# The first group's raw x: two rounded parts kept in DRAM and added later, in place of a copy out of its bank

## The chip, the cores and the metric

The kernel runs on one core of a Trainium2 chip. The metric is the time of one execution on the device in microseconds (us); the median of several executions counts. The engines are named as in the profile: PE (TensorE matmul), PEld (its weight loads), DVE (VectorE), ACT (ScalarE), POOL (GpSimd) and SP (SyncE, which issues every DMA here).

## The reference, cut to what matters

Attention over 4 batches, 8 heads, 768 positions and 64 columns per head: each query sees the keys less than 16 positions away and 24 summary keys (maxima over blocks of 32 keys; their values are means). Its output, laid out as x of 3072 x 512, goes through a two-layer network with softplus:

```python
scores_all = np.concatenate([scores_l_m, scores_s], axis=-1)
a = np.exp(scores_all - np.max(scores_all, axis=-1, keepdims=True))
a = a / (np.sum(a, axis=-1, keepdims=True) + 1e-09)
attn_out = np.matmul(a, np.concatenate([v, v_sum], axis=2))
...
x = np.ascontiguousarray(attn_out.transpose(0, 2, 1, 3)).reshape(B * S, H * D)
h = x @ w_in                                   # 3072 x 512 by 512 x 2048
g = np.maximum(h, 0.0) + np.log1p(np.exp(-np.abs(h)))
return (g @ w_out).astype(np.float32)          # by 2048 x 512
```

## The kernel before

**Groups and passes.** The 3072 tokens form six groups x = 0 to 5 of 512 tokens, each of two chunks i of 256. Attention of a chunk is done for two head pairs at a time (hp = 0 and 2), so a group has four blocks, called a0.0.0, a0.0.2, a0.1.0 and a0.1.2 for group 0 (group, chunk, hp); block n = 2i + hp/2. Groups 0 to 4 first go through the first half of the 16 feed-forward slices (f = 0 to 7, called f0.0 to f0.7 for group 0), group 5 through all of them, and then groups 4, 3, 2, 1, 0 through slices 8 to 15. The second pass uses another product scheme (`hidden_pair`, with sums and differences of the blocks of x), so it needs each group's x again. PE's products take each fp32 operand as two rounded parts (high, and the rest, low) and sum three of the four products.

**Where x goes.** A block's attention output stands in a PSUM bank, xo. For group 0, `attention` does three things with it: ACT or DVE copies the whole bank into an SBUF tile r (the *take*, L767), SP writes r to DRAM (`keep`, L619), and for each of the two columns of heads ACT copies the bank into the high part of xw (L786) and DVE subtracts that from the bank into the low part (L790). The xw tiles of group 0 lie in the tags x3 to x6, which group 2's xw uses next. In the second pass `attended` (L1339) loads the four raw blocks of a group back into r, and `prepare` makes the operands x0 to x6 from them by differences and splits (L796, L803, L811, L812).

**Attention of a block.** PE scores (L646); a DVE mask with the minimum, eight instructions (L659); ACT exponentials, eight (L667); DVE inverse of the sums (L674, L675); normalization by DVE or POOL (L680) or ACT (L683); PE transposes and ACT copies them to pT (L700, L704; for groups 1 to 5 a DVE transpose L713 and a way through DRAM instead); PE values into xo (L746, L754).

**Weights.** Each pair of slices is loaded, rounded and split in a chain per tile: magnitude (DVE L933 or ACT L936), clamp (L940), shift (L944), sign (L948) on DVE, tail (ACT L954 or DVE L957), add of the tail (POOL L962), high (ACT or DVE L966), low (DVE or POOL L973). The first pair, w0, stands in four tiles of 512 columns, wi0_0, wo0_0, wi0_1, wo0_1; later pairs in tiles of 1024.

**What sets the order.** Every piece of work is a task with a number. The string SEQUENCE lists the 2037 tasks in the order in which they are issued, and so the order of each engine's own queue. A letter behind a number (a, b) takes one of the task's other ways, another engine. Each engine works through its queue in order, and SP through its DMAs. The score bank sc is one buffer, xo and ph share two PSUM banks for the hidden products (`bank`, tag ph), and group 0's xo uses the tag po. 40 short matmuls on the identity (L1298) fill PE's opening.

Of the kernel before, what the change touches and what calls it, by code (L numbers as in the profile page):

```python
# [10 lines left out]
F32 = mybir.dt.float32  # L11
# [130 lines left out]
def pool(n):  # L142
    return 0.17 + 0.00219 * n
# [4 lines left out]
23 124 0 125 2 3 25 4 44 47 5 134 161 6 7 24 8 31 27 9 10 126 130 35 11 127 12 128 13 129 14 26 131 33 50 1 132 133a  # L148
51 15 16 52 17 85 18 135 136 66 19 137 20 138 29 21 22 45 82 162 139 37 163 166 53 32 164 54b 165 39 41 67 167 34 284
48 143 68 36 28 55 30 140 57 88 46 168 69 38 49 89 70 40 56 58 90 104 86 180 169 42 84 141a 105 142a 43 106 291 91 59  # L150
309 148a 92a 144 145 146 83 87 147 152 107 170 71 61 108 171 63 62 73 72 292 74 75 334 338 293 149 64 60a 181 93 182
95 183 316 77 79 184 94 96 97 351 76 80 150a 185 120 199 78 294 295a 153a 109 157 154 111 155 110 156 112 113 296 317
158 101 99 100 176 102 151a 159 218 336 115 117 160a 318 297 342 340 116 227 346 98a 118 186 285 121 335 219 339 228
172 173 174 220 319 358 221 229 222 230 223 376 289 337a 114 320b 234 235 224 175 344 286 204 231 177 298 301 299 290
321 241 343 236 287 300 242 187 237 178 341a 225 243 244 226 179 232 288 322 345 359 189 360 233 123 122 239 190 238
245 347 200a 188 302 310 361 383 201 362b 323 348 314 202 240 248 203 468b 472a 205 363 312 313 249 246 303 469b 467
384 326 324 191a 385 325 315 311 255 195a 206a 192 207 364 208 209 256 193 386 194 247 250 251 257 475 252 196 258 327
494b 259 387b 498a 262 349a 365 368 366 263 352 355 328 350 493 356 197a 269 388 367 198a 210a 270 476 353 357 354 495
253 264 211 389 65 643 265 212 214 213 254 271 266 501 272 215 273 369 519 477 260 377 380 216a 217 378 381 261 520a
478 526 521b 390 393 267 370 307 479a 305 308a 306a 372 392 391 382 480 268 373a 329 379 274 502 481 641 278 645 503  # L160
276 330a 332a 333a 277 275 529 394 547 331 548a 549 374a 375 395 399 482 485 484 470 279 397a 398 400 401 402 504 473
483 103 471 474 505 410 403 404 554a 281 282 405 644 506 411 406 412 413 530 507 407 649 647 408 414 409 531 557 486
# [12 lines left out]
762a 631 935a 765 852 763a 837 766 775 635a 767 851 768 875 769 916 876 776 777 940a 770 632 778 633 943 853 877 634
917 879 1028 779 638a 782 542 854a 863 880 639a 1027 636 866 1029 902 771 878 783 918 919a 772 868 869 864 920 944 789
773 945 784 1032a 946 790 785 774 855 735 786 903 780 947 791 792 856 865 781 787 921 881 793 1359 908 904 948 949
1035 882a 1036 1037 1038 1039 922 911 796 797 640 1040 803 804 798 805 914 924 909 1052b 806 799 1056a 858 913 925
1053 800 923 1051 788 794 795 801 637 910 1059 859 807 761 1060 886a 1076 926 936 950 927a 953 942 802 808 809 929
931a 1077a 939 1082a 857a 932 928 810 811 1061 941 1075 884a 885 812 813 937 817 818 814 951 952 815 819 938 1041 1062  # L180
954 820 955 1493 709 1085 1063a 1030 930 816 957a 1360 887a 959 821 1042 956 1045 822 1031 1034 1044 1064 826 960 958a
824 1102 961 825 962 963 1101 970 1033 964 883 829a 1108a 830 971 972 823 1043 973 1065 1086 1103 965 974 1111 1046
1087 827a 1054 966 1047 967 1088 1049 1050 1057 1055 1361a 1089 1048 1066 968 1058 1069 977 978 979 980 984 985 981
986 1090 1112 987 1068 831 969 991 992 993 1494a 988 1067 994 995 1091 975 1070 1365 828 1362 1113 1114 1071 1073 1499
976 1078 1074 1092 1084 982 983 1072 998 999 1495 1093 1005 1000 1095 1369 1001 1115b 989 1079 1081 1080 1083 1002 990
1116 1006 1094 1096 1007 1117 1008 1099 996 1104 997 1106 1009 1105 1012 1366 1097 1118 1013 1372 1003 1014 1110 1121
1015 1016 1120 1100 1109 1107 1496 1004 1119 1010 1503 1098 1500a 1011 1018 1019 1122 1017 1123 1125 1124 1021 1024
1126 1127 1128 1136 1129 1137 1020 1130 1138 1131 1185 1022 1132 1143 1144 1139 1186a 1140 1150 1203 1145 1025 1151
1204 1133 1205 1134 1187 1221 1188 1189 1206 1152 1146 1135 1153 1147 1154 1208a 1141 1207 1226 1194 1157 1142 1164
1165 1158 1222 1199a 1370a 1209 1190 1148 1026 1149 1210 1155 1212 1240 1023 1195a 1223 1224 1196 1225 1213a 1197 1198  # L190
1200 1191 1159 1227 1160 1166 1192 1156 1230 1211 1161 1167 1193a 1168 1171 1172 1241a 1242 1228 1178 1173 1174 1217a
1243 1162 1231 1163 1179 1244 1278 1229 1259 1175 1236 1245 1232a 1233 1214 1169 1234 1201 1235 1180 1246 1181 1170
1182 1295 1260a 1261 1176 1296 1215 1302 1237 1262 1283a 1303 1177 1249 1297 1298 1216 1299 1183 1304 1184 1250 1247
1264 1268 1218 1305 1306 1309 1219 1371a 1310 1316 1202 1263 1238 1248 1265 1220 1311 1312 1317 1300 1255 1318 1301
1266 1239 1307 1308 1269 1313 1279 1280a 1319 1270a 1251a 1320 1267 1323 1281 1252 1253 1274 1324 1254 1325 1326 1327
1330 1271 1256 1314 1331 1272 1337 1332 1373a 1338 1333 1315 1273 1334 1282 1344 1374 1345 1287a 1339 1367 1257 1368
1340 1258 1375 1321 1322 1363 1341 1364 1328 1329 1378 1275 1276 1376 1346 1347 1348 1379 1380a 1501a 1284 1377 1335
1381 1384 1382a 1385 1383 1387 1386 1388 1389 1392 1390 1277 1336 1391 1288 1285 1393 1396 1397 1394 1395 1403 1286a
1342 1404 1343 1349 1351 1289 1502 1398 1405 1408 1290a 1410 1411 1409 1350 1506 1353a 1412 1352 1356a 1417 1414 1357
1415 1419 1399 1413 1420 1418 1358 1421 1354 1400 1509a 1423 1401 1416 1355 1422 1424 1428 1429 1425 1402 1430 1406  # L200
1433 1436 1439 1435 1434a 1437 1440 1438 1442 1441 1444 1446 1291 1407 1426 1445 1443 1627 1448 1447 1449 1453 1454
1497a 1450 1455 1427 1292 1293 1458 1294a 1431 1461 1459 1462 1464 1460 1463 1469 1498a 1465 1467 1471 1466 1470 1468
1472 1473 1478 1479 1504a 1489 1633 1630 1474 1507a 1505a 1432 1451 1452 1508a 1456 1457 1485 1510a 1475 1480 1512
1513a 1637 1511a 1514a 1515 1517 1516 1518 1521 1519 1520 1524 1525 1528 1522 1523 1526 1628 1629a 1476 1477 1527
# [27 lines left out]
def kernel(  # L232
# [9 lines left out]
    nc = tc.nc  # L242
# [379 lines left out]
    def attention(x, i, hp, tiles, by_pe):  # L622
# [136 lines left out]

        order.add(PE, 1.6 if tiles.sums else 1.2, values, [pT, *((pT, k) for k in range(NSQ)), *tiles.v_keys], [xo])  # L760

        r = None
        if x < NX - 1:
            r = block(2 * i + hp // NG)

# [6 lines left out]
            if x:  # L772
                return r
# [623 lines left out]
```

## Time and profile before

| | |
|---|---|
| time, median of 3 runs | 614.34 us (614.16 to 617.19) |
| the profiled execution's own time | 613.83 us |
| its span, first to last instruction | 612.0 us |
| PE busy | 602.7 us (98%) |
| DVE, ACT, POOL busy | 379.3, 343.3, 180.6 us |
| granted TensorE clock | 1.000 |

The profile is that of one execution. A busy engine is one with an instruction in it; PE's matmuls overlap, so a matmul that took 0.39 us on average is followed by the next after 0.23 us. All windows are in us from the first instruction. A number in square brackets behind a timeline row is the idle time of that engine just before, with what ended it.

### The profile page before, as it was taken

The numbers are of one execution on the slowest core, as the hardware profiler recorded it, in microseconds if no ns is written. First come the engines' busy times: TensorE is split into PE (matmuls) and PEld (weight loads), VectorE is DVE, ScalarE is ACT, GpSimd is POOL, SyncE is SP. The second block draws the span as 40 slices with busy tenths as digits, with TensorE's granted clock in tenths as the row PEclk, the third lists the DMA queues.
The fourth block names the chain that finished last, engine by engine and source line by source line (L and its number), as shares of the span: only waits on it lengthen the run. The fifth ranks groups of instructions, "written<-read, shape, count | busy, mean of one in ns | idle before, by whom it ended". The sixth has DMA issues, their size and how long they took to land.

```text
span 612.0 us, 12214 instructions
## 1 busy us (share of the span) xinstructions
PE 602.7 (98%) x4575; PEld 505.6 (83%) x4575; DVE 379.3 (62%) x992; ACT 343.3 (56%) x846; POOL 180.6 (30%) x178
## 2 busy tenths in 40 slices
PE   8899999999999999999999999999999999999997
PEld 7567878888788888888888888899898989999996
DVE  4999987846465665442235689854765655554543
ACT  4989998986778656576266986432213222233211
POOL 4445255134115132210003553572411216012000
PEclk9999999999999999999999999999999999999999
DMA  8999778966868576665428520041040230020121
GB/s 304 310 314 250 236 238 258 280 193 230 263 196 263 175 213 225 213 201 193 135 75 270 206 70 1 1 155 52 2 172 2 103 138 1 35 103 1 48 92 69
DMA packets 66714, 96.13 MB, mean 157 GB/s; under 512 B 5888, under 2 KB 44896, under 8 KB 65888
## 3 DMA queue, kind: packets, MB, share of 16 engines
q1 hardware_dynamic: 66656, 95.36, 48.1%
q8 instruction: 36, 0.59, 0.4%
q14 instruction: 22, 0.18, 0.1%
HBM read 66.06 MB, written 27.26 MB: 152 GB/s over the span
## 4 chain that ended last, share of the span: by engine, by line
PE 86%; DVE 11%; ACT 2%; issue 1%; POOL 0%; DVEq 0%; ACTq 0%; POOLq 0%
PE po L1224 40%; PE ph L1059 21%; PE hx L1099 10%; PE hy L1099 7%; PE xo L746 4%; PE sc L646 3%; DVE sp L659 1%; PE warm L1298 1%; DVE t L948 1%; DVE t L940 1%; DVE ks L352 1%; DVE w L973 1%; DVE gl L1217 1%; DVE tb L713 1%; DVE t L944 1%
## 5 line engine op out<-in xcount | busy, mean ns | idle before, releaser
L1224 PE MATMUL po<-w,gh 128*128 128x512 f32 x766 | 202.7, 392 | 0.3 <-DVE w L973 0.3
L1224 PEld LDWEIGHTS po<-w,gh 128*128 128x128 f32 x766 | 141.0, 188 | 29.6 <-DVE w L973 0.7
L1059 PE MATMUL ph<-xw,w 128*128 128x512 f32 x672 | 161.9, 392 | 0.2 <-POOL w L973 0.2
L1059 PEld LDWEIGHTS ph<-xw,w 128*128 128x128 f32 x672 | 125.1, 188 | 28.1 <-POOL w L973 0.7
L1224 PE MATMUL po<-w,gl 128*128 128x512 f32 x383 | 114.5, 392 | 0.6 <-DVE gl L1217 0.6
L1224 PEld LDWEIGHTS po<-w,gl 128*128 128x128 f32 x383 | 70.7, 188 | 15.3 <-DVE gl L1217 1.0
L667 ACT ACTIVATE sp<-sp,nm 128x120 f32<-128x120 f32 x192 | 73.1, 384 | 5.9 <-DVE nm L659 5.7
L1209 ACT ACTIVATE gh<-hx 128x512 fp32r<-128x512 f32 x20 | 12.0, 600 | 107.6 <-DVE hx L1109 107.6
L962 POOL TENSOR_TENSOR t<-t,raw 128x1024 int32<-128x1024 int32 (+1 forms) x20 | 40.8, 2044 | 103.9 <-DVE t L948 70.0
L1217 DVE TENSOR_TENSOR gl<-ph,gh 128x512 fp32r<-128x512 f32 x56 | 38.2, 686 | 53.0 <-ACT ph L1213 52.8
L1209 ACT ACTIVATE gh<-ph 128x512 fp32r<-128x512 f32 x56 | 33.4, 598 | 37.7 <-PE ph L1059 37.3
L803 POOL TENSOR_TENSOR x<-r,x 128x512 fp32r<-128x512 f32 x23 | 30.5, 1339 | 67.9 <-DVE x L796 58.2
L659 DVE CUSTOM_DVE_ANT_0 sp<-sc,added 128x120 f32<-128x120 f32 x192 | 40.8, 278 | 5.9 <-PE sc L646 4.9
L667 ACT ACTIVATION_READ_ACCUMULATOR sp<-sp,nm 128x1 f32 x192 | 36.2, 189 | 0.0
L1099 PE MATMUL hx<-x,w 128*128 128x256 f32 x240 | 35.7, 285 | 0.0
L1099 PE MATMUL hx<-x,sw 128*128 128x256 f32 x240 | 35.5, 284 | 0.0
L1099 PEld LDWEIGHTS hx<-x,w 128*128 128x128 f32 x240 | 32.9, 190 | 2.1
L1099 PE MATMUL hy<-x,sw 128*128 128x256 f32 x240 | 34.4, 284 | 0.0
L1209 ACT ACT_TABLE_LOAD x23 | 29.5, 1283 | 6.3 <-PE ph L1059 5.9
L1213 ACT ACTIVATE ph<-ph 128x512 f32<-128x512 f32 x56 | 32.9, 591 | 0.0
L1099 PEld LDWEIGHTS hx<-x,sw 128*128 128x128 f32 x240 | 32.0, 190 | 0.8
L1099 PEld LDWEIGHTS hy<-x,sw 128*128 128x128 f32 x240 | 31.2, 191 | 0.2
(122 smaller groups left out, 828.0 us busy)
## 6 DMA issues: line engine op xcount, KB each, us to landing
squares<-tb SPq DMA_DIRECT2D x20, 512.0 KB
pT<-squares SPq DMA_DIRECT2D x80, 128.0 KB
raw<-w_out_dram SPq DMA_DIRECT2D x16, 512.0 KB
kf<-kT_dram SPq DMA_DIRECT2D x16, 384.0 KB
raw<-w_in_dram SPq DMA_DIRECT2D x6, 1024.0 KB
q<-qT_dram SPq DMA_DIRECT2D x20, 256.0 KB
raw<-r SPq DMA_DIRECT2D x20, 256.0 KB
part<-ob SPq DMA_DIRECT2D x10, 512.0 KB
```

Source lines behind the costliest of these rows:

```text
L646: nc.tensor.matmul(unit(g * NU + h * NPAIR + i)[r * QW:(r + 1) * QW, k0:k1], lhsT=q[rows, w * QW:(w + 1) * QW], rhs=k[rows], start=True, s ...
L659: nc.vector.tensor_tensor_reduce(out=sp()[:, n], in0=unit(n), in1=added()[:, kinds.index((lows[w], lows[w + 1]))], scale=-SCALE, scalar=FL ...
L667: nc.scalar.activation(sp()[:, n], sp()[:, n], AF.Exp, bias=nm()[:, n:n + 1], scale=-1.0, accum_out=ss()[:, n:n + 1],)
L746: nc.tensor.matmul(xo()[h * D:(h + 1) * D, g * CH + w * QW:g * CH + (w + 1) * QW], lhsT=v[:, h * D:(h + 1) * D], rhs=queries(g, w, h)[:KW ...
L803: engine.tensor_tensor(to(1), a(), to(0).bitcast(F32), op=ALU.subtract)
L962: nc.gpsimd.tensor_tensor(a, a, word(0, I32), op=ALU.add)
L1059: nc.tensor.matmul(ph(), lhsT=lhs(part, cc), rhs=xw[cc][0]()[:, xw[cc][1], a], start=cc == 0 and n == 0, stop=cc == NCC - 1 and n == 2,)
L1099: nc.tensor.matmul(to()[:, half], lhsT=lhs(wa, cc), rhs=of_x(xa)[:, cc * CH:(cc + 1) * CH], start=cc == 0 and m == 0, stop=cc == NG - 1 an ...
L1209: nc.scalar.activation(gh(), all_of(), AF.Softplus)
L1213: nc.scalar.activation(all_of(), all_of(), AF.Softplus)
L1217: nc.vector.tensor_sub(out=gl(), in0=all_of(), in1=gh().bitcast(F32))
L1224: nc.tensor.matmul((to or po[t])()[:, c0:c1], lhsT=a()[:, t * P:(t + 1) * P], rhs=w2()[:, part, i2 * DM + c0:i2 * DM + c1], start=(f == f0 ...
```

## The change

The take of group 0's four blocks and the four `keep` writes of 256 KB are left out. In their place `keep_parts` writes each of the four xw tiles (high and low parts of both chunks) to DRAM, 512 KB each, and in the second pass `summed` loads, for each block, both parts of two tiles (two DMAs of 256 KB in rows of 1024 B) into a tile named both and adds high and low into r. The tile both takes the tag tb for the blocks n = 0 and 2 and the tag pT for 1 and 3, one buffer each. The four adds are on POOL.

The new SEQUENCE has 2041 tasks; its first 616 positions, which reach to about 155 us of the profile before, are arranged anew, and behind them the order is the old one but for the new loads and adds. Within the stretch up to the low part of the last block of group 0 these are the differences in the queues, read off the numbers:

- PE: 15 instead of 12 of the identity fillers stand ahead of the scores of a0.0.0. The first products of f0.0 stand ahead of the values of a0.1.2, not behind them, and the hidden products of f0.2 ahead of the first projection of f0.0.
- From DVE to ACT: the magnitudes of wi0_0, wo0_0, and of the 1024-wide tiles wi1 and wi2; the high parts of wo0_0 and wi0_1.
- From ACT to DVE: the tail and the high part of wi0_0; from ACT to POOL: the normalization of a0.0.0; later the high part of wo0_1 from ACT to DVE.
- From POOL to DVE: the normalization of a0.1.0 and a0.1.2, the low part of wo0_0, and later that of wo0_1. From DVE to POOL: the normalization of a1.0.0.
- DVE: two of group 1's key maxima (L352) come ahead of the low parts of a0.0.2 and a0.1.2, not behind them.
- ACT: the exponentials of a1.0.2 stand ahead of the high parts of a0.1.2, not behind them.
- SP: the loads of wo0_0 and wo1 are issued later, the last two key loads of group 0 earlier. The writes of the parts stand where the old keeps did, among the DMAs of groups 1 to 3.

```diff
 SEQUENCE = """
-23 124 0 125 2 3 25 4 44 47 5 134 161 6 7 24 8 31 27 9 10 126 130 35 11 127 12 128 13 129 14 26 131 33 50 1 132 133a
+0 23 121 2 3 25 44 47 4 5 6 83 7 27 29 8 9 157 24 10 11 12 13 122a 123 31 126a 14 15 33 124 16 17 26 125 127 80 50
...
-        r = None
-        if x < NX - 1:
+        if 0 < x < NX - 1:
             r = block(2 * i + hp // NG)
...
-            if x:
-                return r
+            return r
         xw = whole_x(x)
...
-        return r
+
+    first_parts = {}
+
+    def keep_parts(cc):
+
+        buf, i = whole_x(0)[cc]
+        first_parts[cc] = to = buffer([P, 2, CT], F32, f"parts{cc}", pool=dram, bufs=1)
+        order.add(
+            SP, 0, lambda: nc.sync.dma_start(out=to(), in_=buf()[:, i].bitcast(F32)),
+            [(buf, i, part, k) for part in range(2) for k in range(2)], [to], size=512 * KiB, row=4096,
+        )
+
+    def summed(n, r):
+        i, hp = n // 2, n % 2 * NG
+        both = buffer([P, 2, NG, CH], F32, "both", ("tb", "pT")[n % 2], 1, work)
+        for g in range(NG):
+            def load(g=g):
+                src = first_parts[hp + g]()
+                nc.sync.dma_start(out=both()[:, :, g], in_=src[:, :, i * CH:(i + 1) * CH])
+            order.add(SP, 0, load, [first_parts[hp + g]], [(both, g)], size=256 * KiB, row=1024)
+
+        def add(engine):
+            to = r().rearrange("p (g c) -> p g c", g=NG)
+            engine.tensor_tensor(to, both()[:, 0], both()[:, 1], op=ALU.add)
+        order.add(
+            POOL, pool(NG * CH), lambda: add(nc.gpsimd), [(both, g) for g in range(NG)], [r],
+            ways=[Way(DVE, dve(NG * CH), lambda: add(nc.vector), port=True)],
+        )
...
-            n = 2 * i + hp // NG
-            keep(0, n, attention(0, i, hp, tiles, True))
+            attention(0, i, hp, tiles, True)
+        for cc in range(hp, hp + NG):
+            keep_parts(cc)
...
-            def load(n=n):
-                nc.sync.dma_start(out=r[n](), in_=kept(x, n)())
-            order.add(SP, 0, load, [kept(x, n)], [r[n]], size=256 * KiB, row=2048)
+            if x:
+                def load(n=n):
+                    nc.sync.dma_start(out=r[n](), in_=kept(x, n)())
+                order.add(SP, 0, load, [kept(x, n)], [r[n]], size=256 * KiB, row=2048)
+            else:
+                summed(n, r[n])
             prepare(x, n, r)
```

## Rows read from the trace of the kernel before

**Rows 1.** Busy us of PE, PEld, DVE, ACT, POOL by stage; clock, DMA share, GB/s.
```profile
0.00:43.00 43.00, 39.13 (x629) 27.94 (x630) 33.96 (x129) 32.90 (x114) 17.56 (x35) 1.00 0.96 313
43.00:50.00 7.00, 6.77 (x57) 4.68 (x58) 6.82 (x26) 6.02 (x22) 5.82 (x4) 1.00 1.00 290
50.00:78.00 28.00, 26.88 (x277) 21.76 (x269) 27.24 (x68) 26.27 (x73) 9.78 (x7) 1.00 0.80 237
78.00:350.00 272.00, 272.00 (x2113) 222.28 (x2112) 153.57 (x485) 193.45 (x499) 72.87 (x81) 1.00 0.67 212
390.00:600.00 210.00, 210.00 (x1310) 189.56 (x1309) 118.09 (x239) 56.31 (x106) 57.01 (x45) 1.00 0.19 66
```

**Rows 2.** Timeline of the opening: start, us, engine, line, operation, [idle before].
```profile
6.08 0.43 DVE L933 TENSOR_SCALAR t<-raw 128x512 uint32<-128x512 uint32 x1 [1.36 <-DMA raw<-w_in_dram]
...
8.40 1.29 POOL L962 TENSOR_TENSOR t<-t,raw 128x512 int32<-128x512 int32 x1 [2.65 <-DVE t L948]
...
9.79 0.42 PE L646 MATMUL sc<-kf,first 64*64 64x96 f32 x8
...
11.35 0.28 DVE L659 CUSTOM_DVE_ANT_0 sp<-sc,added 128x120 f32<-128x120 f32 x1 [2.33 <-PE sc L646]
```

**Rows 3.** Timeline of PE, the first hidden products and the first projection.
```profile
42.89 2.11 PE L1059 MATMUL ph<-xw,w 128*128 128x512 f32 x8
...
52.01 0.50 PE L1224 MATMUL po<-w,gl 128*128 128x512 f32 x1 [0.56 <-DVE gl L1217]
52.35 0.63 PE L1059 MATMUL ph<-xw,w 128*128 128x512 f32 x2
```

**Rows 4.** Timeline of DVE, 27 to 49 us.
```profile
27.99 0.38 DVE L957 TENSOR_SCALAR raw<-raw 128x512 int32<-128x512 uint32 x1
...
34.34 0.68 DVE L767 COPY r<-xo 128x512 f32<-128x512 f32 x1
34.94 0.69 DVE L933 TENSOR_SCALAR t<-raw 128x1024 uint32<-128x1024 uint32 x1
...
38.59 0.42 DVE L966 CAST w<-t 128x512 fp32r<-128x512 f32 x1
...
39.69 1.16 DVE L680 TENSOR_TENSOR sp<-sp,ss 128x960 f32<-128x960 f32 x1
...
46.30 0.68 DVE L767 COPY r<-xo 128x512 f32<-128x512 f32 x1
46.90 0.41 DVE L790 TENSOR_TENSOR xw<-xo,xw 128x256 fp32r<-128x256 f32 x1
47.23 1.80 DVE L352 TENSOR_REDUCE ks<-kf 128x24 f32<-128x768 f32 x2
```

**Rows 5.** Timeline of ACT, 37 to 49 us.
```profile
37.46 0.60 ACT L767 COPY r<-xo 128x512 f32<-128x512 f32 x1
...
48.16 1.28 ACT L1209 ACT_TABLE_LOAD   x1
```

**Rows 6.** Groups by line and shape, 20 to 55 us: count | busy us, mean ns | idle before.
```profile
L667 ACT ACTIVATE sp<-sp,nm 128x120 f32<-128x120 f32 x38 | 14.5, 386 | 0.0
...
L680 POOL TENSOR_TENSOR sp<-sp,ss 128x960 f32<-128x960 f32 x2 | 3.6, 1791 | 5.0 <-DVE ss L675 5.0
```

**Rows 7.** Timelines of DVE, then of POOL, around 360 us.
```profile
358.06 0.68 DVE L973 TENSOR_TENSOR w<-t,w 128x512 fp32r<-128x512 f32 x1
...
359.80 5.76 DVE L973 TENSOR_TENSOR w<-t,w 128x1024 fp32r<-128x1024 f32 x3
...
360.02 3.31 POOL L962 TENSOR_TENSOR t<-t,raw 128x1024 int32<-128x1024 int32 x1 [1.84 <-issue]
```

**Rows 8.** Timelines of POOL, then of SP, in the second pass.
```profile
490.34 1.30 POOL L812 TENSOR_TENSOR r<-r 128x512 f32<-128x512 f32 x1
510.19 2.54 POOL L803 TENSOR_TENSOR x<-r,x 128x512 fp32r<-128x512 f32 x2 [18.55 <-DVE x L796]
...
475.99 1.38 SPq L1339 DMA_DIRECT2D r<-raw  x3
```

More of the change, by code (lines that the diff above doesn't have):

```diff
@@ L153 @@
[L153 to L162, printed above, removed]
@@ new lines @@
+260 78 261 210 491a 208 209 250 267 262 497 211 268 269 365 515 473 256 386 373 374 387 389 212a 213 388 378 376 257
+377 301a 326a 474 263 366 375 368 475a 303 328 329a 516b 522a 264 476 517b 637 304a 370 643 498 273 270 271 499 477
+302a 272 525 390 543 544a 545 327 277 550 278a 466 467 470 391 639 395 393a 394 396 371a 369a 397 398 274a 500 501 478
+479 480 406 399 400 407 401 502 526 469 481 413 402 414 408 640 641 409 275a 503 645 527 649 410 403 415 404 405 482
+638 528 553 504 507 654 642 411 655b 416 661 529a 492 495 505 412 506 418 496 656b 483a 417 487a 485 493 530 554 531
@@ new lines @@
+419 420 421 555 646 279 647 508 556 557 422 664 683 532 535 509 423 425 533 392 518 523 521 424 644 558 665 520 682
+534 524 519 666 427 434 486a 559 428 651 684a 667 115 114 435 426 429 436 430 431 432 650 437 438 536 560 668a 689a
+692 546 548 552 563 441 442 561 562 669 648 652a 551 547 537a 541a 539a 653 693 711a 715 433 513 443 444 712a 445 549
+540 439 710 367 670 440 694 446 564 657 718 736 695 488 696a 448 565 569 542a 697 737b 741 738b 300 449 671 511a 512
+567 568 570a 719 450 276 659 514a 571 451 572 452 447 573 574 453 456 457 454 455 484 672 325 674 580 581 460a 886 458
@@ new lines @@
+679 624 732a 845 929 897 625 837 462 870b 832 626 735 707a 709a 756a 760a 681 733 930b 846 836 834 758a 627 931a 761
+848 759a 833 762 771 631a 763 847 764 871 765 912 872 772 773 936a 766 628 774 629 939 849 873 630 913 875 1024 775
+634a 778 538 850a 859 876 635a 1023 632 862 1025 898 767 874 779 914 915a 768 864 865 860 916 940 785 769 941 780
+1028a 942 786 781 770 851 731 782 899 776 943 787 788 852 861 777 783 917 877 789 1355 904 900 944 945 1031 878a 1032
+1033 1034 1035 918 907 792 793 636 1036 799 800 794 801 910 920 905 1048b 802 795 1052a 854 909 921 1049 796 919 1047
@@ new lines @@
+965 987 988 989 1490a 984 1063 990 991 1087 971 1066 1361 824 1358 1109 1110 1067 1069 1495 972 1074 1070 1088 1080
+978 979 1068 994 995 1491 1089 1001 996 1091 1365 997 1111b 985 1075 1077 1076 1079 998 986 1112 1002 1090 1092 1003
+1113 1004 1095 992 1100 993 1102 1005 1101 1008 1362 1093 1114 1009 1368 999 1010 1106 1117 1011 1012 1116 1096 1105
+1103 1492 1000 1115 1006 1499 1094 1496a 1007 1014 1015 1118 1013 1119 1121 1120 1017 1020 1122 1123 1124 1132 1125
+1133 1016 1126 1134 1127 1181 1018 1128 1139 1140 1135 1182a 1136 1146 1199 1141 1021 1147 1200 1129 1201 1130 1183
@@ new lines @@
+1305 1215 1367a 1306 1312 1198 1259 1234 1244 1261 1216 1307 1308 1313 1296 1251 1314 1297 1262 1235 1303 1304 1265
+1309 1275 1276a 1315 1266a 1247a 1316 1263 1319 1277 1248 1249 1270 1320 1250 1321 1322 1323 1326 1267 1252 1310 1327
+1268 1333 1328 1369a 1334 1329 1311 1269 1330 1278 1340 1370 1341 1283a 1335 1363 1253 1364 1336 1254 1371 1317 1318
+1359 1337 1360 1324 1325 1374 1271 1272 1372 1342 1343 1344 1375 1376a 1497a 1280 1373 1331 1377 1380 1378a 1381 1379
+1383 1382 1384 1385 1388 1386 1273 1332 1387 1284 1281 1389 1392 1393 1390 1391 1399 1282a 1338 1400 1339 1345 1347
@@ new lines @@
+1513 1512 1514 1517 1515 1516 1520 1521 1524 1518 1519 1522 1624 1625a 1472 1473 1523 1627a 1480 1526 1479 1477 1525
+1533 1534 1527 1528 1535 1538 1541 1630 1482 1486 1544 1539a 1542 1487 1540 1547 1478 1543 1631a 1545 1529 1483 1549
+1632 1548 1550 1530 1551 1552 1553 1546 1554 1558 1559 1555 1531 1532 1560 1536 1537 1563 1564a 1569 1566 1567 1565
+1570 1568 1571 1574 1572 1576 1573 1575 1556 1577 1578 1639a 1579 1580 1636 1557 1583 1584 1585 1561 1588 1594 1589
+1591 1597 1590 1562 1592 1598 1599 1593 1640 1641 1595 1601 1602 1596 1581 1600 1582 1603 1637a 1608 1634a 1628a 1488
@@ new lines @@
+1907 1908 1718 1909 1719 1722 1618 1725 1723 1724 1731 1728 1726 1691 1733 1622 1727 1732 1774a 1768 1894 1695 1735
+1775a 1895a 1729 1771 1777a 1736 1734 1730 1737 1738 1696 1715 1716 1720 1899a 1739 1778a 1769a 1742 1743 1744 1772
+1779 1781 1782 1785 1780a 1783 1721 1786 1784 1790 1788 1787 1789 1904a 1791 1792 1753 1793 1740 1741 1794 1795 1796
+1801 1802 1746 1803 1747 1806 1807 1754 1749 1751 1808 1815 1809 1816 1810 1745 1750 1752 1811 1748 1817 1812 1819
+1813 1818 1814 1755 1821 1822 1912a 1820 1823 1826 1827 1797 1905 1798 1799 1828 1800 1804 1831 1837 1832a 1834 1833
```

101 lines of the change are left out of this document (38 added, 63 removed), and 12 rows, old and new, of the table SEQUENCE.

## The prediction

> **What bounds the kernel now.** I read the busy time by stage first [rows 1]. PE is busy for all 272 us between 78 and 350 us and for all 210 us between 390 and 600 us, while DVE and ACT have room there (154 and 193 of 272 us). The reader is to see that a microsecond taken from DVE or ACT in those stretches is worth nothing. The exception is the opening: the first hidden product starts at 42.89 us [rows 3], and until then PE's 39.1 busy us of 43 [rows 1] are partly the identity fillers. From about 20 to 78 us DVE is the engine without room: 6.82 of 7 and 27.24 of 28 us [rows 1], ACT close behind. So I read PE's timeline for the start of the hidden products [rows 3], then the queues of DVE and ACT to see what they hand over late [rows 4, 5], and the opening for where DVE itself waits [rows 2]. After 78 us PE carries any delay to the end unchanged: the forecast is the shift of PE at 78 us.
>
> **Takes, keeps and parts.** Of the four takes two are on DVE, at 34.34 and 46.30 us, each 0.60 us from its start to the next one's (rows overlap by some 0.08 us, so I count starts), and two on ACT, one of 0.60 us at 37.46 [rows 4, 5]. They are the gain: 1.2 us of DVE and about 1.1 of ACT before 78 us. The keeps are SP issues of about 0.46 us each (1.38 for three DMAs of that size [rows 8]); four go, four of twice the size come, so 1 MB more is written, at a DMA share of 0.67 [rows 1], long after xw was made. I cost them at nothing: group 2's first writes into these tiles, which must now wait for the parts' landing, come some tens of us after the last hidden product of f0 has read them. If that cover is gone, ACT's high part waits, and behind it in ACT's queue the next softplus, then PE.
>
> **DVE's queue to the last low part of a0.1.2.** This is what f0.0's second half waits for; before, it ends at 46.90 + 0.41 = 47.31 us [rows 4]. Leaving it: the takes, 1.20; four magnitudes, two of 0.72 (34.94 to 35.66) and two of 0.46, together 2.36; two casts of 512 columns at 0.33, 0.66; the normalization of a1.0.0, 1.08. Sum 5.3. Entering: two normalizations, 2 x 1.08; a tail, 0.29; a cast, 0.33; the low part of wo0_0, 0.60; two maxima ahead of the lows, 2 x 0.87 [rows 4, 7]. Sum 5.1. So the work is the same within 0.2 us: what the takes free is filled.
>
> **DVE's waits.** Before, the opening has one of 1.36 us and one of 2.33 [rows 2], and smaller ones make it some 4.5. After: ACT makes the first magnitude from 6.08 us, 0.70, so the clamp starts at 6.8, and DVE idles from 4.7 to 6.8 (2.1). With tail, shift, a maximum and the sign (0.3 + 0.5 + 0.9 + 0.7) the sign ends near 9.75, where it ended 0.24 us ahead of POOL's 8.40 before; POOL's 1.29 follows [rows 2], and the cast on DVE waits for it until 11.3 (1.6). Three more fillers of 0.43 us move the first scores from 9.79 to 11.08, and the mask from 11.35 to 12.64 (0.9). Later the high of a0.1.0 and POOL's normalization of a1.0.0 (1.79, [rows 6]) add 0.3 each, small ones 0.2. In all 5.4, so 0.9 more; less the 0.2, the last low part ends near 48.0 us, 0.7 late.
>
> **ACT.** Its exponentials cost 14.5/38 x 8 = 3.05 us a block [rows 6]. Four magnitudes and two casts come in; a normalization of eight instructions, a tail, two casts and the takes go: about even. The order puts the exponentials of a1.0.2 ahead of a0.1.2's high parts: these end near 46.5, just before DVE gets to them. On SP the loads of wo1 now stand behind a load of q that waits for the scores of a1.0.2, near 37 us, some 6 us later than before; ACT and DVE first read wo1 near 47, so I cost it at nothing.
>
> **PE.** f0.0's first half can start near 41 us, ahead of a0.1.2's values, against 42.89; but f0.1's second half ends 0.7 late, near 50.2. Then f0.2's products stand ahead of f0.0's projection and need the bank that f0.0's low part frees: after a table load of 1.28 us [rows 5], two softplus passes and DVE's subtraction that is 52.5, a wait of 1.0 us where the old order waited 0.56 [rows 3]. The old order has by then done one projection (0.7 us) more, and starts f0.2 at 52.35 [rows 3] against 52.5 here, so PE is 0.9 late. From there to 78 us DVE is not later still: the two maxima (1.7) and a tail of 1024 columns (0.6) are gone from behind the lows, a low part and a cast of wo0_1 (0.9) come in, and DVE stands about 1.2 us at that subtraction. The sum is 0.9 us.
>
> **The second pass.** Four POOL adds of 1.30 us. POOL is done at 491.6 and then idle for 18.55 us [rows 8]; two of them stand in front of the row at 490.34. The tile both has one buffer for two blocks, so SP holds the third and later loads until POOL has added the first block, near 491.7, and the last pair until about 498; behind these in SP's queue stand an output of the group before and two reloads of partial sums, which are wanted only when that group's slices are through. Cost nothing; POOL's gap of 18.55 us less 5.2 of adds and some 6 of loading leaves about 7 us before it would cost.
>
> [...]
>
> [...]
>
> **Rivals.** *B, the takes' time comes through.* If DVE's early waits stay at 4.5 us, then the 0.9 does not arise, and if the bank wait is covered PE keeps the 1.2 us of DVE and part of ACT's 1.1: 614.3 - 2.2 = 612.1, at best 610.5. For it: the first hidden half is 1.9 us earlier. Against it: DVE's sum. *C, the block of exponentials is exposed.* ACT stands at a1.0.2's exponentials until DVE's mask comes; if that mask starts more than 2 us after its 42.5 us, the whole 3.05 us delays f0's operands: 614.3 + 0.9 + 3.05 = 618.3, slower. POOL's normalization just ahead of it speaks for, its otherwise idle queue against. [...] *E, a late landing of the parts* stops ACT in front of a softplus near 133 us: more than 4 us late is needed, then 1 to 3 us; I count it with C.
>
> **The numbers.** The profiled execution took 613.83 us, 1.8 more than its span of 612.0, and stands 0.5 below the median; the sum is a difference, put on the median: 614.3 + 0.9 = 615.2. My case, between 613.4 and 617.2 (the upper end is the 3.0 us low part on DVE), has a chance of 0.52, B 0.26, C with E 0.17, D 0.05; mine is also the case in which the change frees takes and gains nothing by it. Half a per cent, 3.1 us, is what can be told from no change. Half of B, 0.13, is beyond it; of C, D and E 0.17; the rest, 0.70, is within. For eight in ten the range reaches into B and C: 611.7 to 618.4.
>
> **What would show it.** In the new profile: the mask of a0.0.0 near 12.6 us, DVE's last low part near 48, the first hidden product near 41 with PE waiting 1 to 2 us before f0.0's second half, another 1 us near 52, and PE without idle time from 80 us on; SP's part loads spread from 476 to 499. Wrong would be a last low part before 46.5 (B), a mask of a1.0.2 after 44.5 (C), or PE idle in the second pass (D).

## The result, and the profile after

The changed kernel takes 618.2 us, the median of 20 executions (615.64 to 624.41), against 614.19 us for the kernel before in the same runs: 1.0075 times the time, with a 95% interval of 1.0059 to 1.0091. It is slower by 0.75%. The forecast was 615.2 us and, with a chance of 0.70, a change too small to be told from none; 618.2 lies just inside the range (611.7 to 618.4), but at 4.0 us the change can be told. Of the experiments below, five executions that took over 1.5% longer than the fastest of their kernel are left out of every figure: one of hyb72_fillers, two of four_fillers_less and two of eight_fillers_less.

The profiled execution took 616.54 us, with a span of 614.7 against 612.0. The stages [rows 1] are now these:

```profile
0.00:43.00 43.00, 39.12 (x590) 28.59 (x591) 33.90 (x131) 31.24 (x107) 18.22 (x34) 0.92 0.93 286
43.00:50.00 7.00, 7.00 (x62) 5.11 (x61) 6.15 (x21) 6.97 (x24) 2.73 (x3) 1.00 0.96 330
50.00:78.00 28.00, 27.99 (x303) 22.82 (x304) 26.13 (x69) 27.34 (x74) 9.93 (x7) 1.00 0.79 245
78.00:350.00 272.00, 270.09 (x2097) 219.75 (x2092) 154.41 (x486) 188.64 (x487) 68.50 (x74) 1.00 0.68 215
390.00:600.00 210.00, 210.00 (x1311) 189.61 (x1310) 120.44 (x240) 55.22 (x105) 63.95 (x50) 1.00 0.21 71
```

Two things stand there that the forecast did not have. Between 78 and 350 us PE is idle for 1.9 us, where it had no idle time. And in the first stage the granted clock is 0.92, not 1.00. From 43 to 78 us, the stretch on which the forecast was built, PE waits less than before, not more.

I followed the same product of the hidden layer through both traces. The first of f0.6 starts at 78.70 us, 0.2 us earlier than before (78.89). The first of f1.0 starts at 100.29 (99.97), its second half at 103.06 (101.44), f1.6 at 138.32 (135.82), and the same projection (`po`) near the end of the second pass at 602.74 (599.84). So PE is ahead at 78 us (and 0.4 us at 91), is 2.5 us late at 138 us, and carries that to the end with 0.4 more.

The waits of PE between 80 and 142 us (before, there is none over 0.2 us) name the places:

```profile
PE ph L1084 <- POOL xw L859: 1.0, 1, 1.0
PE po L1249 <- ACT gh L1234: 0.5, 1, 0.5
PE sc L646 <- ACT sp L667: 0.4, 1, 0.4
```

That is 1.9 us of idle time. Counted from a matmul's start to the next one's start, less the 0.23 us of one at full pace, the three stops cost 1.26, 0.70 and 0.55 us: 2.5 of the 2.9.

The first, in the timelines of PE and of POOL:

```profile
98.23 1.05 PE L646 MATMUL sc<-k,q 64*64 64x120 f32 x32 [0.38 <-ACT sp L667]
...
100.29 0.50 PE L1084 MATMUL ph<-xw,w 128*128 128x512 f32 x1
101.78 2.60 PE L1084 MATMUL ph<-xw,w 128*128 128x512 f32 x10 [0.98 <-POOL xw L859]
...
94.80 2.14 POOL L859 TENSOR_TENSOR xw<-r,xw 128x256 fp32r<-128x256 f32 x3 [4.51 <-ACT xw L852]
99.45 0.71 POOL L512 COPY k<-kf 128x288 f32<-128x288 f32 x2 [2.50 <-ACT sp L667]
100.12 1.60 POOL L859 TENSOR_TENSOR xw<-r,xw 128x256 fp32r<-128x256 f32 x2
```

POOL is idle for 2.50 us in front of a copy of keys (L512) into the window tile k, which has one buffer. The profile puts this wait down to ACT's exponentials; in the old order it puts the same copy's wait, of only 0.31 us, down to PE's scores:

```profile
99.12 0.72 POOL L512 COPY k<-kf 128x288 f32<-128x288 f32 x2 [0.31 <-PE sc L646]
```

The scores of the block before read the tile k. In the new order they start at 98.23 us, after PE's wait of 0.38 us for ACT's exponentials, and end at 99.28; the copy follows at 99.45. (The expectation of lows_ahead below speaks of a copy of q that waits for its load. That is a misreading: the load is issued at 99.33 us, just ahead of the copy's start, and behind the same scores.) Behind that copy stand the two low parts of a1.1.0 that f1.0 needs; their high parts were there from 96.30 us. In the old order one of the two ran on POOL at 95.72 and the other on DVE at 100.02. The wait for ACT is of the same kind, in ACT's timeline:

```profile
127.81 1.28 ACT L667 ACT_TABLE_LOAD   x1 [2.39 <-DVE nm L659]
...
132.27 1.28 ACT L1234 ACT_TABLE_LOAD   x1
133.56 1.09 ACT L1234 ACTIVATE gh<-ph 128x512 fp32r<-128x512 f32 x2
```

The mask of a3.0.0 comes late on DVE (127.44 us, before 125.80), the exponentials end at 132.15, and a second table load lies ahead of the softplus that PE waits for at 133.7 us.

The clock, by windows of the opening (PE, PEld, DVE, ACT and POOL busy, then clock, DMA share, GB/s):

```profile
26.00:30.00 4.00, 3.94 (x108) 3.08 (x108) 3.93 (x12) 3.95 (x16) 0.12 (x2) 1.00 1.06 304
30.00:32.00 2.00, 0.80 (x8) 0.55 (x6) 2.00 (x4) 1.98 (x10) 0.00 (x0) 1.00 1.02 269
32.00:34.00 2.00, 1.85 (x38) 1.51 (x40) 2.00 (x18) 2.00 (x6) 1.30 (x1) 0.97 1.11 290
34.00:38.00 4.00, 4.00 (x57) 3.08 (x56) 3.93 (x10) 4.00 (x18) 0.00 (x0) 0.50 0.88 235
38.00:40.00 2.00, 2.00 (x52) 1.95 (x47) 1.97 (x6) 2.00 (x5) 1.00 (x1) 0.50 0.03 8
40.00:42.00 2.00, 2.00 (x27) 1.34 (x24) 1.52 (x2) 0.98 (x3) 2.00 (x2) 0.82 0.96 311
```

PE is idle for 1.35 us ahead of 32.15 us, and from 33.9 to 40.7 us the granted clock is 0.50. The 20 executions differ in this. In six the mean clock is 0.999 or more, and their median is 617.2 us; in the six with 0.990 or less it is 622.8 us. The kernel before had 0.999 or more in 68 of 77 executions in this study. So about 3.0 us of the 4.0 are there at full clock (617.2 against 614.2), and the executions at a lower clock add 1.0 to the median. Those are the nine at 0.992 or less, with a median of 620.1 us. The five at 0.994 to 0.997, the profiled one among them, have a median of 616.5 us and show no cost of the fall. What brings the clock down is shown only in part: PE's idle time in the first 43 us is the same in both kernels (3.9 us, first lines of the stages).

### The profile page after: what moved, and what is told of

The parts are those of the page before. It is cut to its first block, busy times and chain, and to the rows that moved or that the text cites. A ratio compares the mean times of both kernels' runs of the same rounds, so it can differ in the third digit from the quotient of the medians.

```text
span 614.7 us, 12206 instructions
## 1 busy us (share of the span) xinstructions
PE 604.8 (98%) x4575; PEld 507.4 (83%) x4575; DVE 382.0 (62%) x994; ACT 341.8 (56%) x834; POOL 179.4 (29%) x174
## 2 busy tenths in 40 slices
DMA packets 68314, 98.23 MB, mean 160 GB/s; under 512 B 5952, under 2 KB 47008, under 8 KB 67488
## 4 chain that ended last, share of the span: by engine, by line
PE 75%; ACT 12%; DVE 6%; DMA 2%; POOL 2%; issue 1%; SPq 0%; DVEq 0%; POOLq 0%; ACTq 0%
PE po L1249 33%; PE ph L1084 17%; PE hx L1124 9%; PE hy L1124 7%; ACT sp L667 4%; PE xo L746 3%; PE sc L646 3%; DMA raw<-w_out_dram 2%; PE warm L1323 2%; ACT L961 1%; ACT t L961 1%; ACT L1234 1%; ACT raw L979 1%; ACT w L991 1%; ACT gh L1234 1%
## 5 line engine op out<-in xcount | busy, mean ns | idle before, releaser
L659 DVE CUSTOM_DVE_ANT_0 sp<-sc,added 128x120 f32<-128x120 f32 x192 | 40.7, 277 | 4.4 <-PE sc L646 3.5
L680 POOL TENSOR_TENSOR sp<-sp,ss 128x960 f32<-128x960 f32 x10 | 18.1, 1815 | 66.3 <-DVE ss L675 52.0
```

Of the source, the lines that this page charges most:

```text
L659: nc.vector.tensor_tensor_reduce(out=sp()[:, n], in0=unit(n), in1=added()[:, kinds.index((lows[w], lows[w + 1]))], scale=-SCALE, scalar=FL ...
```

## The experiments

All times are medians. "At full clock" means the executions with a mean granted clock of 0.999 or more.

| kernel | us | ratio to before, 95% interval | at full clock | their median, us |
|---|---|---|---|---|
| changed | 618.2 | 1.0075 (1.0059 to 1.0091) | 6 of 20 | 617.2 |
| parts_old_order | 616.9 | 1.0049 (1.0024 to 1.0073) | 6 of 7 | 616.4 |
| takes_new_order | 623.9 | 1.0152 (1.0134 to 1.0170) | 0 of 4 | |
| lows_ahead | 618.8 | 1.0067 (1.0042 to 1.0092) | 2 of 11 | 615.2 |
| three_fillers | 617.5 | 1.0067 (1.0040 to 1.0095) | 6 of 8 | 617.1 |
| mended | 617.3 | 1.0037 (1.0008 to 1.0066) | 5 of 7 | 615.5 |
| parts_at_keeps | 621.0 | 1.0095 (1.0074 to 1.0116) | 0 of 6 | |
| hyb72 | 622.7 | 1.0138 (1.0123 to 1.0152) | 0 of 4 | |
| hyb72_fillers | 622.6 | 1.0132 (1.0112 to 1.0151) | 0 of 4 | |
| parts_early | 613.9 | 0.9984 (0.9966 to 1.0002) | 11 of 12 | 614.0 |
| takes_new_order_fillers | 621.4 | 1.0109 (1.0069 to 1.0149) | 4 of 7 | 620.9 |
| mended_reloads | 617.5 | 1.0044 (1.0021 to 1.0067) | 9 of 12 | 616.6 |
| four_fillers_less | 616.6 | 1.0040 (1.0009 to 1.0071) | 4 of 9 | 614.5 |
| eight_fillers_less | 617.3 | 1.0055 (1.0022 to 1.0088) | 0 of 10 | |

Theory 1 was the waits of the new order behind 95 us, theory 2 the clock, theory 3 the parts themselves.

**parts_old_order.** The changed kernel's functions, the old order of tasks (renumbered), and the writes of the parts put in as two pairs, here `79 78` and `115 114`:

```diff
+389 263 366 303 475a 301 304a 302a 368 388 387 378 476 264 369a 325 375 270 498 477 115 114 637 274 641 499 272 326a
```

> The change's computation (no takes, the parts written and added) in the order of the kernel before; the first pair of part writes stands behind the same SP instruction as in the changed kernel, the second pair some 30 us earlier. Theory 1 (the new order of the first 616 positions costs the time, above all PE's wait for a POOL low part at 100 us and for ACT at 134 us): 612.5 to 614.5 us, nothing lost, no PE idle time over 0.3 us between 90 and 140 us that the kernel before has not. Theory 2 (the granted clock falls in the opening, because PE idles more there): no fall, so the same as theory 1. Theory 3 (the parts themselves cost: 2 MB more of writes and reads, and their issues in SP's queue hold the loads behind them): 616.5 to 618.5 us.

616.9 us, with the clock up: theory 3's figure. Its six executions at full clock spread from 614.7 to 620.2 us, and the profiled one is the slowest of them. In it, all but 0.2 us of PE's waits between 80 and 142 us are for loads:

```profile
PE xo L746 <- DMA pT<-squares: 2.7, 2, 1.9
PE xo L746 <- DMA v<-v_hp_dram: 1.5, 1, 1.5
PE sc L646 <- DMA q<-qT_dram: 0.8, 1, 0.8
PE po L1249 <- ACT gh L1234: 0.2, 1, 0.2
```

The first pair stands on SP at 86.06 us, just behind the write of a transposed block; that block's third reload is issued at 95.01 us, where it was 92.89. The second pair stands at 100.55 us. (The changed kernel has a first pair at nearly the same place, 86.75 us, and there PE waits for no load.) What this leaves open is whether the bytes cost or their place.

**takes_new_order.** The kernel before in the new order:

```diff
-23 124 0 125 2 3 25 4 44 47 5 134 161 6 7 24 8 31 27 9 10 126 130 35 11 127 12 128 13 129 14 26 131 33 50 1 132 133a
+0 23 125 2 3 25 44 47 4 5 6 85 7 27 29 8 9 161 24 10 11 12 13 126a 127 31 130a 14 15 33 128 16 17 26 129 131 82 50
...
```

> The computation of the kernel before (takes and keeps, no parts) in the changed kernel's new order; each take stands behind the first low part or the first transposed copy of its block, as in the kernel before. Theory 1: 617 to 619.5 us, PE waits again 1 us or more near 100 us for a low part on POOL. Theory 2: 616 to 620 us, with a granted clock below 0.995 in some executions. Theory 3: 613.5 to 615 us.

623.9 us, more than any theory said, all four executions at a clock of 0.989 to 0.992. Without a single part, PE waits at the same places by the same amounts, though it comes there 5 us later:

```profile
PE xo L746 <- DVE gl L1217: 1.0, 1, 1.0
PE ph L1059 <- POOL xw L834: 1.0, 1, 1.0
PE po L1224 <- ACT gh L1209: 0.5, 1, 0.5
PE sc L646 <- ACT sp L667: 0.4, 1, 0.4
```

So the waits for POOL and ACT belong to the new order, not to the parts.

**lows_ahead.**

```diff
-302a 272 525 390 543 544a 545 327 277 550 278a 466 467 470 391 639 395 393a 394 396 371a 369a 397 398 274a 500 501 478
+302a 272 525 390 543 327 544a 371a 369a 545 277 466 467 470 391 639 395 393a 394 396 550 278a 397 398 274a 500 501 478
```

> The changed kernel with six words of the order moved: the two low parts of a1.1.0 stand on POOL ahead of the copy of q that waits for its load, the low part of a1.0.2 stands on DVE ahead of its half of that copy, and two copies on DVE stand behind the low parts of a1.1.2. Theory 1: PE does not wait within f1.0 any more and is 1.3 to 1.6 us earlier from 103 us on; 616.3 to 617.0 us by median. Theory 2: 618.2 us, since the clock's opening is untouched. Theory 3: 618 us, the waits go elsewhere.

The edit moves five words. PE's wait for POOL is gone, as theory 1 said:

```profile
PE xo L746 <- DVE gl L1242: 0.5, 1, 0.5
PE po L1249 <- ACT gh L1234: 0.5, 1, 0.5
PE sc L646 <- ACT sp L667: 0.4, 1, 0.4
PE po L1249 <- DVE w L998: 0.2, 1, 0.2
```

But PE's idle time between 78 and 350 us is 2.0 us in this profile (an execution with a mean clock of 0.991), where it was 1.9: other waits, 0.5 us for DVE the longest, stand in its place. The median did not move, 618.8 us; nine of eleven executions ran below full clock. The two at full clock took 614.91 and 615.46, 2.0 us under the changed kernel's 617.2, but they are only two; the five below 0.993 had a median of 621.0.

**three_fillers.** The new words stand ahead of the values of a0.1.0; later words are renumbered.

```diff
-    for _ in range(20):
+    for _ in range(23):
```

> The changed kernel with three more identity products on PE just ahead of the values of a0.1.0, where PE is idle for 1.35 us at 30.8 us. Theory 1: the wait near 100 us is untouched; 616.8 to 617.5 us by median, since only the executions with a low clock gain. Theory 2 (the fall of the clock makes the loss): the granted clock stays at 1.00 between 33 and 42 us, and the time comes to 614 to 615 us. Theory 3: 618 us.

Six of eight executions ran at full clock, where it had been six of twenty, and there the time is 617.1 us: theory 1's figure. In its profile f0.0 starts 2.2 us earlier than before, and PE has lost all of it at 103 us (1.8 us late). This profile is at full clock throughout, and PE is idle there for 3.3 us between 78 and 350 us:

```profile
78.00:350.00 272.00, 268.67 (x2067) 218.37 (x2067) 153.39 (x484) 186.67 (x482) 67.40 (x73) 1.00 0.69 214
```

**mended.** `lows_ahead`, the transpose 558 ahead of 424, and seven fillers.

> The changed kernel with the moves of lows_ahead, with one transpose of a2.1.2 on DVE ahead of f1.3's subtraction (so that the next mask, exponentials and softplus come earlier: the wait for ACT at 134 us), and with seven more identity products on PE: two ahead of the scores of a1.0.0, three ahead of the values of a0.1.0, two ahead of the scores of a1.0.2. Theory 1 and 2 together (the new order's waits after 95 us, and the clock's fall after PE's idle time in the opening, make the whole loss): clock 0.999 or more in most executions, no PE wait at 100 and 134 us, 614.0 to 615.0 us. Either alone: 616 to 617 us. Theory 3 (the parts' writes): 617 us, PE waits for loads.

The wait for POOL and that of 0.5 us for ACT are gone (one of 0.4 us for ACT's exponentials stays), the clock is up in five of seven, and at full clock the median is 615.5 us, 1.6 better than the changed kernel, though the five spread from 614.9 to 619.1. It is not the 614 to 615 that I expected. PE came to a1.1.0's values 1.1 us ahead and then waited there 1.5 us for a transposed block in DRAM, and 0.8 us more near 214 us for another.

**parts_at_keeps.** Each part in the place of one keep, in the order 79, 78, 115, 114 (the lines of SEQUENCE that hold them):

```diff
+258 345a 361 364 362 259 348 351 324 346 489 352 193a 265 384 363 194a 206a 266 472 349 353 350 491 249 260 207 385 79
...
+271 525 390 543 327 544a 545 370a 371 391 395 478 481 480 466 275 393a 394 396 397 398 500 469 479 78 467 470 501 406
...
+647 648 420 556 421 557a 422 664 682 423 424 508 509 518 521 532 115 427 434 428 419 425 426 558 665 520 535 533 523
...
+650 513 666 514a 485a 683 689a 519 524 534 559 435 429 436 430 431 437 438 684b 432 667 668b 692 711a 710 114 536 537a
```

> As parts_old_order, but each of the four part writes stands where one of the four keeps stood, none of them two together behind a transposed block's write. Theory 3a (in parts_old_order it was the pair of writes just behind the block's write that held its reloads up, so the place costs and not the bytes): 613.5 to 614.8 us, no PE wait for a load over 0.5 us between 95 and 120 us. Theory 3b (2 MB where 1 MB was cost wherever they stand): 616.5 to 617.5 us. Clock 0.999 or more in both.

621.0 us, neither theory. Until 130 us PE ran 0.8 us ahead of the kernel before without a wait for a load, so the pairs and their place were indeed what cost in parts_old_order. Then rival E came, in the order where I had not looked for it: a part was issued at 123.86 us, and ACT's rounding of a2.0.2 over the same tile waited for its landing (the first of ACT's waits, 95 to 140 us):

```profile
ACT xw L852 <- DMA parts<-xw: 4.7, 1, 4.7
```

PE stands behind it, by windows:

```profile
130.00:132.00 2.00, 1.21 (x6) 0.67 (x4) 0.00 (x0) 2.00 (x12) 0.00 (x0) 1.00 0.80 315
132.00:134.00 2.00, 0.00 (x0) 0.00 (x0) 0.00 (x0) 1.97 (x5) 0.00 (x0) 1.00 0.01 2
134.00:136.00 2.00, 1.64 (x6) 1.29 (x7) 0.68 (x2) 2.00 (x6) 0.00 (x0) 0.82 0.00 0
136.00:138.00 2.00, 2.00 (x18) 1.25 (x19) 0.89 (x4) 1.26 (x5) 0.00 (x0) 0.50 0.00 0
```

PE is idle for 3.15 us, and then works at a granted clock of 0.50: 5 us in all, from 0.8 ahead to 4.2 behind.

**hyb72 and hyb72_fillers.** The new order up to the first product of f0.5, then the old one as in parts_at_keeps; the second with mended's fillers.

> The changed kernel's order up to the first hidden product of f0.5 (72 us), behind it all that is left in the order of the kernel before, with the parts where the keeps stood. Theory 1 (the loss lies behind 78 us): 613.5 to 614.8 us in the executions with a clock of 0.999 or more, and 3 to 6 us more in those below 0.992, so a median of 615 to 617 us. If the opening itself lost the time: 617 us or more at full clock too.

> hyb72 with the seven identity products of mended. Theory 1 and 2: clock 0.999 or more in most executions, 613.3 to 614.6 us by median, level with the kernel before. If the fillers themselves delay the opening: 615 us or more at full clock.

622.7 and 622.6 us. Both carry the same late part (issued at 126.0 us in hyb72, where PE waits 4.6 us for ACT and the granted clock is 0.69 from 134 to 138 us and 0.50 from 138 to 142), so they say nothing of the end. Up to 119 us hyb72 is 1.2 us behind the kernel before, after being 0.4 ahead at 83 us: even with the old order behind 72 us something of the new one is still missed in that stretch. They were no test of theory 1.

**parts_early.** The four places of parts_at_keeps with the parts in the order in which they are overwritten: the words 115 and 79 change places. Against parts_at_keeps:

```diff
-258 345a 361 364 362 259 348 351 324 346 489 352 193a 265 384 363 194a 206a 266 472 349 353 350 491 249 260 207 385 79
+258 345a 361 364 362 259 348 351 324 346 489 352 193a 265 384 363 194a 206a 266 472 349 353 350 491 249 260 207 385
+115 639 261 208 210 209 250 267 262 497 268 211 269 365 515 473 256 373 376 212a 213 374 377 257 516a 474 522 517b 386
...
```

> As parts_at_keeps, with the same four places but the parts in the order in which group 2 overwrites their tiles: the one that the first rounding of a2.0.2 on ACT waited 4.74 us for now stands at 86 us instead of 124. Theory: in the order of the kernel before the change gains what the takes free, PE runs 0.8 us ahead from 83 us to the end (as parts_at_keeps did until 130 us), the clock stays at 0.999 or more, and no wait of 1 us or more stands between 95 and 140 us: 613.2 to 613.9 us. Rival (twice the bytes written cost somewhere whatever the places): 614.5 us or more.

613.9 us, and eleven of twelve executions at full clock. Its stages:

```profile
43.00:50.00 7.00, 7.00 (x88) 5.11 (x86) 6.90 (x26) 6.97 (x24) 4.73 (x3) 1.00 1.01 304
50.00:78.00 28.00, 26.74 (x256) 21.91 (x256) 27.24 (x67) 25.97 (x73) 11.11 (x7) 1.00 0.77 233
78.00:350.00 272.00, 271.73 (x2084) 221.67 (x2082) 153.59 (x484) 192.58 (x495) 71.58 (x81) 1.00 0.70 216
```

It is the same computation, with the same 2 MB of parts, as the changed kernel, which takes 4.3 us more. PE is 1.4 us ahead of the kernel before at 57 us, 1.1 at 100 us and 0.3 at the end. It is the fastest version of the study, level with the kernel before within the interval. The new order with its parts in these places was not run, so how much of the changed kernel's loss comes from its own two pairs (86.75 and 132.38 us) stays open; takes_new_order shows that the new order loses time without any part.

**takes_new_order_fillers.** takes_new_order with mended's seven fillers.

> takes_new_order (the kernel before with its takes and keeps, in the new order) with the seven identity products of mended, so that the clock has less cause to fall. Theory (the new order costs 2.5 to 3.5 us behind 85 us by its own waits, without any parts): 616.5 to 618.5 us in the executions with a clock of 0.999 or more, the waits of 1.2 us for POOL near 100 us and 0.7 us for ACT near 134 us unchanged. Rival (the new order costs through the clock alone): 614 to 615 us in those executions.

At full clock 617.4 to 622.6 us, and the waits of 1.0 for POOL and 0.5 for ACT unchanged. The new order costs without the clock and without the parts; by more than I expected, since in the profiled execution (622.6 us) waits of 0.6 us near 49 us and of 2.1 near 217 came to it, and stalls of 1.8 us in the opening (last section).

**mended_reloads.** One reload, 369 here, ahead on SP, against mended:

```diff
-496 260 255 261 330 390b 262 352a 265 355 358 368 331 266 371 353 370 359 360 497b 200a 501a 391 201a 272 369 356 479
+496 260 255 261 330 390b 262 352a 265 355 358 368 331 266 371 369 353 370 359 360 497b 200a 501a 391 201a 272 356 479
```

> mended with one reload of a1.1.0's transposed block moved on SP from behind three loads to just behind its sister (it was issued at 84.8 to 84.9 us in three executions of the new order, at 79.7 to 80.8 us in the old one). If that reload is what keeps PE's values of a1.1.0 from starting before 88 us: they start near 87 us with a wait under 0.5 us, PE stays 0.8 us ahead, 614.0 us. If the loads as a whole fill the DMA there: the wait stays at 1 to 1.8 us and the time at 615 to 617 us.

The values of a1.1.0 now start without a wait, so it was this reload that they waited for. But those of a1.0.2 had waited 1.8 us ahead of 78.33 us, and the time is 617.5:

```profile
PE xo L746 <- DVE gl L1242: 1.8, 1, 1.8
```

This wait is for DVE and not for a load: DVE's subtraction `gl`, which frees a bank, ends at 78.27 us. A wait of 1.0 us for a reload stays near 213 us. The 14 executions at full clock of mended and mended_reloads, which both have the moves of lows_ahead, have a median of 616.6 us, only 0.6 under the changed kernel's. So where the new order's waits lie is well shown, and what taking the first ones away is worth is not: PE then comes sooner to others.

**four_fillers_less and eight_fillers_less.** parts_early without its last four or eight identity products; nothing of the output hangs on these. Against parts_early, with four less:

```diff
-    for _ in range(20):
+    for _ in range(16):
```

> parts_early without the last four of the twenty identity products, those on PE between 13.6 and 15.6 us; nothing else waits for them. If PE's idle time in the opening is what the granted clock falls after: PE idle for 1.9 us there, a clock below 0.996 in more executions than the 1 in 12 of parts_early, and those executions 2 to 6 us longer. If it isn't: 0.999 or more in all and 613.9 us.

> parts_early without the last eight of the twenty identity products (10.2 to 12.2 and 13.6 to 15.6 us), so that PE is idle for some 4 us in the opening. [...]

Full clock in four of nine executions and in none of ten, where parts_early had eleven of twelve. With four less, the executions at full clock take 614.5 us and those below 0.993 a median of 620.2. In the order in which the clock had stayed up, taking fillers out of PE's opening is enough to bring it down. The 6 us between the two groups are not the clock's alone: in the profile they hold a stall of 3.43 us as well. And not every fall costs so much: with eight less, five of the ten executions have a clock of 0.994 to 0.997 and take 614.6 to 615.4 us, and the five at 0.989 or less take 619.2 to 623.6. The windows of four_fillers_less:

```profile
26.00:28.00 2.00, 1.11 (x39) 0.81 (x39) 1.97 (x16) 1.95 (x10) 0.72 (x1) 1.00 1.06 286
28.00:30.00 2.00, 0.21 (x8) 0.11 (x3) 1.93 (x4) 2.00 (x12) 0.00 (x0) 1.00 0.93 250
30.00:32.00 2.00, 0.36 (x9) 0.36 (x13) 1.04 (x4) 0.28 (x2) 0.75 (x1) 0.52 0.40 90
32.00:36.00 4.00, 4.00 (x62) 3.34 (x57) 0.00 (x0) 0.00 (x0) 2.27 (x2) 0.50 0.32 94
36.00:40.00 4.00, 4.00 (x40) 3.01 (x37) 2.55 (x19) 2.58 (x9) 0.00 (x0) 0.50 1.00 348
40.00:42.00 2.00, 2.00 (x23) 1.37 (x22) 1.90 (x4) 2.00 (x12) 0.00 (x0) 0.92 0.94 324
```

In PE's timeline the idle time ahead of the fall ends with this row:

```profile
31.64 0.30 PE L646 MATMUL sc<-ks,q 64*64 64x24 f32 x1 [3.43 <-issue]
```

While PE runs at a granted clock of 0.50, DVE and ACT are empty from 32 to 36 us (0.00 us busy each, PE 4.00 of 4). The idle time ahead of the fall is not the missing fillers' own, though, but a stall of 3.43 us later on (last section); why fewer fillers should bring that on is not shown, and kernels with more of them have it too (three_fillers, 1.4 us). With eight less a first fall, to 0.50 from 13.7 to 17.1 us, does follow the fillers' own gap.

## Why the prediction was wrong

**The step that failed** is the one on which the forecast was put: "After 78 us PE carries any delay to the end unchanged: the forecast is the shift of PE at 78 us." It is a statement about the old order [rows 1], and I used it for a new one that reaches to about 155 us. I read the new queues up to the low parts of group 0 and stopped. The loss is made where I did not read: 2.9 us between 91 and 138 us, 2.5 of it at three stops in which PE waits for POOL's queue and ACT's. takes_new_order shows these waits without the parts, lows_ahead takes the largest away by moving five words (other waits come in its place), and parts_early, the same computation in the old order, has none of them and loses nothing. PE's 272 us without idle time spoke of a slack that the old order had there; the new order had spent it.

**The second miss** is that the clock stands in no step. I took PE's waits in the opening as delays only, and the fillers as filling; that the clock can fall to half for 7 to 14 us behind them (0.50 from 33.9 to 40.7 us in the changed kernel, from 30.7 to 44.4 in eight_fillers_less) I did not weigh. The executions in which it falls longest add 1.0 us to the median, and the slowest is 7 us over the median at full clock; how much of that is the clock and how much the idle time ahead of it the times don't tell. The shorter falls, with a mean clock of 0.994 to 0.997, show no cost here.

**DVE's queue.** Right in size: the mask of a0.0.0 starts at 12.03 us (forecast 12.6), the last low part ends at 48.48 (forecast 48.0; it was 47.31, [rows 4]), in an execution with the clock low from 33.9 us. What the takes free is filled again, in the new order. The upper end of the range, 617.2, was put on a low part of 3.0 us on DVE. No run shows that for the two that moved there: they take 0.68 us (at 31.15) and 0.69 (at 50.18). The one low part of 512 columns near that length, 2.94 us, is in both traces, at 360.93 us before and at 363.83 after.

**PE in the opening.** The first hidden product starts at 42.56 us, not 41; in mended, at full clock, it starts at 40.93, so the step was right and the low clock hid it. The waits of 1 to 2 us ahead of f0.0's second half and of 1.0 near 52 us are not there: a0.1.2's values, at 44.13, fill the first, and f0.2 starts at 51.98 against 52.5 forecast and 52.35 before [rows 3]. At 78 us PE is 0.2 ahead where I had it 0.9 late.

**Takes, keeps and parts.** That they cost nothing holds for the bytes (parts_early) but not for any place: the two pairs of parts_old_order cost 2 us of the median at full clock, and one part issued 1.3 us after ACT had come to overwrite it costs 5. The takes are worth 1.4 us at 57 us in the profile of parts_early and 0.3 at the end, which can't be told from nothing.

**The second pass.** Right: PE is busy for 210.00 of 210 us, the four adds take 1.28 to 1.31 us each, and rival D, PE idle in the second pass, is out. One DVE subtraction (L836), at 503.10 us beside the third add, takes 1.50 us where the same one at 488.12 takes 0.69, and PE does not wait for it. The times were off: the last loads are issued at 505 us and not 499, and the adds run from 493.21 to 508.29 us, none of them ahead of the row at 490.34 [rows 8]; it costs nothing all the same. **Rivals.** B did not come, for the order and not for DVE's sum. C's 618.3 is hit by accident: its mask starts at 42.21 us, before the 44.5 from which it decides. E stands in the changed kernel as a wait of 1.3 us on ACT that PE does not feel; its mechanism was shown where I misplaced the part, and its price there is 5 us, where I had 1 to 3.

## What to carry to other kernels

Where an order written out by hand is arranged anew, read every queue to the last position that moved, and not only to where the old profile stops having room: "no idle time" in the old trace is a property of the old order. Change the computation and the order in separate steps, since here the first alone, in the old order, can't be told from nothing (613.9 us with the parts well placed, 616.9 and 621.0 with them badly placed), and the second costs 4 us. And look at the granted clock and its spread over executions when PE's idle time in the opening is moved: two kernels whose profiles have the same sum of it had full clock in 68 of 77 executions and in 6 of 20.

## What was not expected of the hardware

PE stops without a reason that the profile shows. In 8 of the 15 traces PE is idle for 0.7 to 3.4 us within the scores of a1.0.0 with "issue" as the reason, that is, waiting for nothing that the profile shows: 3.4 us in four_fillers_less, 2.5 in eight_fillers_less, 1.7 in takes_new_order, 1.4 in three_fillers, and 0.7, the shortest, in lows_ahead. The queue q8, of kind "instruction", carries 36 packets and 0.59 MB over the whole span. In four_fillers_less one of these packets passes between 29 and 31 us, in the middle of the stop, and none from 16.8 to 29 us; in parts_early, which doesn't stop, one passes between 24 and 26 us. The queues in these two windows, the first of four_fillers_less, the second of parts_early (packets, MB, share of the 16 engines):

```profile
q1 hardware_dynamic: 407, 0.30, 66.7%
q8 instruction: 1, 0.02, 3.9%
```

```profile
q1 hardware_dynamic: 635, 0.49, 124.2%
q8 instruction: 1, 0.02, 4.0%
```

That PE's stop hangs on this packet is not shown: no run moved the packet alone. Why it passes some 5 us later in the one kernel than in the other the traces don't show either; that in four_fillers_less the DMA is at a share of 1.06 from 26 to 28 us is in the windows above.

And the clock falls in the middle of the kernel as well: after the 3.15 us of idle time ahead of 134.36 us in parts_at_keeps it is at 0.50 from 135.3 to 138.7 us.
